# The swap of q's halves on GpSimd instead of SyncE's DMA queue, in a fused attention and ELU-MLP kernel

## The chip, the core and the metric

The kernel runs on one NeuronCore of one Trainium2 chip. The core has five engines with an instruction stream each: PE (TensorE, matmuls into PSUM), DVE (VectorE), ACT (ScalarE), POOL (GpSimd) and SP (SyncE, which here issues every DMA). Each engine works through its stream in order and waits on semaphores for the others. The metric is the device time of one execution in microseconds; less is better.

## The reference

Attention over 8 batches, 12 heads, 448 rows and 64 columns per head, with an RMS norm on q and k, followed by a two-layer MLP with ELU over the 3584 rows of 768 columns.

```python
def _attn_ref(q, k, v, g_q, g_k):
    q_n, k_n = (rmsnorm(q, g_q), rmsnorm(k, g_k))
    scores = 1.0 / np.sqrt(q.shape[-1]) * np.matmul(q_n, k_n.transpose(0, 1, 3, 2))
    attn = np.exp(scores - np.max(scores, axis=-1, keepdims=True))
    attn = attn / (np.sum(attn, axis=-1, keepdims=True) + 1e-09)
    return np.matmul(attn, v).astype(np.float32)

def _moe_ref(x, w_in, w_out):
    h = x @ w_in
    g = np.where(h > 0.0, h, np.exp(np.minimum(h, 0.0)) - 1.0)
    return (g @ w_out).astype(np.float32)
```

## The kernel before

The inputs are fp32. Every matmul operand is split into a high and a low fp16 part, so that a product is made of three fp16 products added up in PSUM.

**Pairs of heads.** The 12 heads of a batch are 6 pairs, 48 pairs in all, counted p = 0 to 47. The 896 rows of a pair (2 heads of 448) are cut into 7 tiles of 128 rows, counted T over the whole kernel. For a pair, `load_qk` (line 338) loads q and k, `qk_norm` (line 386, POOL) scales them, `k_high` and `q_high` (ACT) round them to fp16, `k_low` and `q_low` (line 414 and 421, POOL) make the rests. The high part lies in columns 0 to 63 and the rest in columns 64 to 127 of a tile of 128 columns, so that the DMA transpose of `qk_transpose` (line 429) puts high parts into partitions 0 to 63 and rests into partitions 64 to 127 of `qkt[p]`. That tile has three slots of 128 x 896 fp16: slot 0 is q, slot 1 is k, and slot 2 is q again with the two halves of the partitions exchanged. `q_swap` (lines 433 to 436) makes slot 2 out of slot 0.

**Scores.** `s_mm` (line 528) makes the scores of tile T with slot 0 against slot 1 (high times high and rest times rest in one pass) and then with slot 2 against slot 1 (the mixed products), added in the same PSUM bank. So the first tile of a pair needs the transposes for its first matmul and the swap for its second. Four PSUM banks (`s`) go round. For each T follow `s_max` (DVE, line 542), `s_exp` (ACT, 548), `s_z` (POOL, 552: a tiny instruction on the sum), `s_rec` (DVE, 559), `s_hi` (ACT, 566), `s_lo` (DVE, 571), and `s_tr` (line 581), the DMA transpose of the probabilities into `pt`. `attend` (line 592) multiplies them with v: 22 matmuls per pair.

**Weights and MLP.** `conv_in` and `conv_out` split the weights w_in (16 pieces) and w_out (24 pieces) into fp16 parts on the way; they take ACT, DVE, POOL (lines 282, 313, 322) and PE time during about the first quarter of the span. `v_mult`, `v_high`, `v_low` and `v_shift` (lines 440 to 459, POOL) prepare v. `v_shift` copies between partitions 0 to 63 and 64 to 127 on POOL: two copies of 64 x 384 fp16 per pair. The matmuls of the MLP (lines 677 and 691) begin when the first batch has its attention output, and are woven between the attention's instructions.

**Order.** The loop over half steps h (line 768) writes the order of all engines out: two half steps per tile T, 14 per pair. `at` (line 702) puts a helper's call at a half step; the MLP's matmuls are dealt out at a fixed rate (`RATE`). For p > 1 the transposes of q and of k stand at steps 4 and 6 of the pair in front, `q_swap` at 8, `v_mult` at 9. In that order the instructions reach each engine's stream; a wait of an instruction holds up all behind it on its engine.

Of the kernel before, what the change touches and what calls it, by code (L numbers as in the profile page):

```python
# [32 lines left out]
def tile_attention_then_elu_mlp(ctx: ExitStack, tc: tile.TileContext, qk, v, v_scan, gg, w_in, w_out, out):  # L33
# [13 lines left out]
    nc = tc.nc  # L47
# [15 lines left out]
    def t_mo():  # L63
# [8 lines left out]
        out=neg, in0=ident, scalar1=-1.0, scalar2=None, op0=ALU.mult  # L72
# [3 lines left out]
        out=ident, in0=ident, scalar1=2.0**UP, scalar2=None, op0=ALU.mult  # L76
# [356 lines left out]
    def q_swap(p):  # L433
        q = qkt[p]
        for a, z in ((64, 0), (0, 64)):
            nc.sync.dma_start(out=q[z : z + 64, 2], in_=q[a : a + 64, 0])

    def v_mult(p):
        n = vn[p]
# [280 lines left out]
    for p in range(NP):  # L720
        hb = HP * (p - 1)
        steps = (-20, -14, -12, -10, -8, -4, -1, -1, 1, 4, 2)
        steps = early.get(p) or [hb + h for h in steps]
        for h, fn in zip(steps, (
            load_qk, qk_square, qk_sum, qk_root, qk_newton, qk_norm, k_high, q_gain, q_high, k_low,
            q_low,
        )):

            at(-3 if p == 2 and fn == load_qk else h, fn, p)
        for h, i in ((4 if p > 1 else 6, 0), (6 if p > 1 else 8, 1)):  # L730
            at(hb + h, qk_transpose, p, i)
        at(hb + 8, q_swap, p)
        h0 = HP * p
        for h, fn in ((-2, load_v), (9, v_mult), (10, v_high), (11, v_low), (12, v_shift)):
            at(h0 + h + (5 if (p == 0) == (h > 0) and p < 2 else 0), fn, p)
        at(h0 + 22, x_high, p)
        at(h0 + 23, x_low, p)
# [125 lines left out]
```

## Time and profile before

| | |
|---|---|
| time, median of 3 runs | 1286.1 us (1285.51 to 1286.39) |
| the profiled execution | 1287.73 us, its span 1285.6 us |
| PE busy | 1191.8 us, 93% of the span |
| DVE busy | 853.3 us, 66% |
| ACT busy | 878.7 us, 68% |
| POOL busy | 529.4 us, 41%, 843 instructions |
| chain that ended last | PE 79%, ACT 6%, DVE 5%, POOL 4%, issue 3%, DMA 2% |
| swaps (line 436) | 96 DMAs of 112 KB, 2.4 us from issue to landing (median) |
| transposes of q and k (line 429) | 96 DMAs, 3.1 us from issue to landing (median) |

The span is the time from the first to the last instruction. The share of an engine is taken over the whole span, although its stages have different limits: the strip of 40 slices below shows PE at 30 to 80% in the first nine slices (one is 32 us) and at 90% or more from there on. In it a digit is the busy share in tenths, and PEclk the granted TensorE clock in tenths of full speed.

```
PE   3676578889999999999999999999999999999998
POOL 3675775665334333343344433434334334420000
PEclk9878679999999999999999999999999999999999
DMA  8999898899877897889787986799787977663011
```

### The profile page before, as it was taken

The page shows a single profiled execution, that of the slowest core. Times are in us where ns is not written, and L with a number is a line of the kernel's source. Part 1 is how long each engine was busy: PE and PEld are TensorE (multiplying, and loading weights), DVE is VectorE, ACT ScalarE, POOL GpSimd, SP SyncE. Part 2 cuts the span into 40 slices and gives each one's busy share as a digit, 9 for nine tenths or more (in the row PEclk, how much of TensorE's full clock was granted, in tenths as well). Part 3 has the DMA queues.
Part 4 walks back from the last instruction along what each step waited for, and adds up shares of the span by engine and source line. Part 5 has one row for each costly group of instructions (what it writes and reads, how often), then busy time and mean ns, then how long its engine had stood idle before and what let it go on. Part 6 is the DMA issues. An engine that isn't in the chain of part 4 may idle for free.

```text
span 1285.6 us, 21501 instructions
## 1 busy us (share of the span) xinstructions
PE 1191.8 (93%) x6976; PEld 716.4 (56%) x6976; DVE 853.3 (66%) x1913; ACT 878.7 (68%) x1889; POOL 529.4 (41%) x843
## 2 busy tenths in 40 slices
PE   3676578889999999999999999999999999999998
PEld 1333234456655765576556665576557755666576
DVE  7878779886677557856677567856785668642310
ACT  6887778985788558855797478855886578743520
POOL 3675775665334333343344433434334334420000
PEclk9878679999999999999999999999999999999999
DMA  8999898899877897889787986799787977663011
GB/s 274 224 215 239 199 224 181 199 205 236 175 147 154 203 197 142 164 166 223 149 164 157 215 176 148 155 197 203 139 169 166 219 152 171 133 147 87 1 47 62
DMA packets 452560, 219.22 MB, mean 171 GB/s; under 512 B 408673, under 2 KB 428769, under 8 KB 452449
## 3 DMA queue, kind: packets, MB, share of 16 engines
q1 hardware_dynamic: 452448, 217.86, 78.2%
q8 instruction: 55, 0.90, 0.3%
q14 instruction: 57, 0.46, 0.1%
HBM read 93.52 MB, written 14.16 MB: 84 GB/s over the span
## 4 chain that ended last, share of the span: by engine, by line
PE 79%; ACT 6%; DVE 5%; POOL 4%; issue 3%; DMA 2%; SPq 0%; ACTq 0%; POOLq 0%; DVEq 0%
PE mo L691 32%; PE mo L677 30%; PE s L535 8%; PE av L592 7%; DMA pt<-p 2%; PE mo L289 1%; ACT w32s L225 1%; ACT wts L224 1%; POOL nat L391 1%; ACT s L548 1%; POOL whi L282 1%; DVE wts L230 1%; DVE gall L571 1%; DVE st L542 1%; DVE gall L632 1%
## 5 line engine op out<-in xcount | busy, mean ns | idle before, releaser
L677 PE MATMUL mo<-x,whi 128*128 128x448 f16 x1536 | 422.8, 352 | 5.0 <-DVE e L624 5.0
L691 PE MATMUL mo<-gall,whos 128*128 128x448 f16 x1536 | 422.8, 353 | 0.7 <-DVE gall L632 0.7
L542 DVE TENSOR_REDUCE st<-s 128x1 f32<-128x448 f32 x336 | 208.4, 620 | 176.2 <-PE s L535 175.4
L552 POOL TENSOR_SCALAR st<-st 128x1 f32<-128x1 f32 x336 | 77.3, 230 | 552.4 <-ACT s L548 544.5
L691 PE MATMUL mo<-gall,wls 128*128 128x448 f16 x768 | 271.9, 354 | 0.0
L677 PE MATMUL mo<-x,wli 128*128 128x448 f16 x768 | 270.9, 353 | 0.0
L566 ACT ACTIVATE p<-s,st 128x448 f16<-128x448 f32 x294 | 185.6, 631 | 119.2 <-DMA pt<-p 99.9
L691 PEld LDWEIGHTS <-whos 128*128 128x128 f16 x1536 | 221.6, 145 | 72.3
L548 ACT ACTIVATE s<-s,st 128x448 f32<-128x448 f32 x336 | 203.2, 605 | 61.4 <-DVE st L542 58.4
L535 PE MATMUL s<-qkt 128*128 128x448 f16 (+1 forms) x768 | 188.8, 365 | 53.3 <-DVE gall L571 39.3
L677 PEld LDWEIGHTS <-whi 128*128 128x128 f16 x1536 | 150.2, 98 | 143.1 <-issue 6.9
L571 DVE SCALAR_TENSOR_TENSOR p<-s,st,p 128x448 f16<-128x448 f32 x294 | 196.4, 668 | 30.5 <-ACT p L566 28.5
L691 PEld LDWEIGHTS <-wls 128*128 128x128 f16 x768 | 110.4, 144 | 43.0 <-issue 8.4
L535 PEld LDWEIGHTS <-qkt 128*128 128x128 f16 (+1 forms) x768 | 63.2, 101 | 124.3 <-issue 62.4
L632 DVE SCALAR_TENSOR_TENSOR gall<-e,gsc,gall 128x448 f16<-128x448 f32 x128 | 100.8, 787 | 24.4 <-ACT gall L629 24.2
L677 PEld LDWEIGHTS <-wli 128*128 128x128 f16 x768 | 75.1, 98 | 74.7 <-issue 7.5
L592 PE MATMUL av<-pt,vt 128*64 128x448 f16 x1056 | 113.0, 362 | 0.1
L629 ACT ACTIVATE gall<-e,gsc 128x448 f16<-128x448 f32 x128 | 85.1, 665 | 24.3 <-DVE e L624 24.3
L599 ACT ACTIVATE x<-av 128x448 f16<-128x448 f32 x48 | 26.1, 543 | 104.4 <-PE av L592 104.4
L620 ACT ACTIVATE e<-e,nisc,isc 128x448 f32<-128x448 f32 x128 | 96.9, 757 | 0.3
L616 ACT ACTIVATE e<-mo,sc 128x448 f32<-128x448 f32 x128 | 80.6, 630 | 22.3 <-PE mo L677 22.0
L624 DVE SCALAR_TENSOR_TENSOR e<-e,mo 128x448 f32<-128x448 f32 x128 | 78.5, 613 | 16.6 <-ACT e L620 11.9
(100 smaller groups left out, 1372.6 us busy)
## 6 DMA issues: line engine op xcount, KB each, us to landing
wls<-wl_d SPq DMA_DIRECT2D x48, 512.0 KB, 3.9
nat<-in_qk SPq DMA_DIRECT2D x48, 448.0 KB, 3.9
raws<-in_w_out SPq DMA_DIRECT2D x24, 512.0 KB, 4.4
qkt<-qkt SPq DMA_DIRECT2D x96, 112.0 KB, 2.4
out<-y SPq DMA_DIRECT2D x48, 224.0 KB, 2.9
vn<-in_v SPq DMA_DIRECT2D x38, 256.0 KB, 3.7
vscan<-in_v_scan SPq DMA_DIRECT2D x36, 224.0 KB, 3.9
whos<-in_w_in SPq DMA_DIRECT2D x10, 768.0 KB, 5.5
```

Source lines behind the costliest of these rows:

```text
L535: nc.tensor.matmul(ps[r0 : r0 + n, :S], lhs, qq[:, 1, h * S : h * S + S], start=(t == 0), stop=(t == 2),)
L542: nc.vector.tensor_reduce(out=st[:, 0:1], in_=pss[T][:, :S], axis=AX.X, op=ALU.max, negate=True)
L548: nc.scalar.activation(ps, ps, AF.Exp, bias=st[:, 0:1], accum_out=st[:, 1:2])
L566: nc.scalar.activation(p16[:, :S], pss[T][:, :S], AF.Copy, scale=stats[T][:, 2:3])
L571: nc.vector.scalar_tensor_tensor(out=p16[:, S:], in0=ps[:, :S], scalar=r, in1=p16[:, :S], op0=ALU.mult, op1=ALU.subtract)
L592: nc.tensor.matmul(av[64 * h : 64 * h + 64, :S], vt[p][:, j + NJ * i, h], pt[h][:, j, :], start=(k == 0), stop=(k == len(terms) - 1),)
L616: nc.scalar.activation(e, ph[:, :S], AF.Exp, scale=sc)
L620: nc.scalar.activation(e, e, AF.Identity, scale=isc, bias=nisc)
L629: nc.scalar.activation(g[:, 0], e, AF.Copy, scale=gsc)
L632: nc.vector.scalar_tensor_tensor(out=g[:, 1], in0=e, scalar=gsc, in1=g[:, 0], op0=ALU.mult, op1=ALU.subtract)
L677: nc.tensor.matmul(ph[:, :S], w[:, c, :], x[:, r, :], start=(c == 0 and i == 0), stop=last)
L691: nc.tensor.matmul(py[:, :S], w, g[:, r, :], start=(f == 0 and i == 0), stop=last)
```

## The change

`q_swap` makes slot 2 with two copies on POOL, 64 partitions x 896 columns of fp16 each, where it issued two DMAs within SBUF on SP. The half step at which it stands is unchanged.

```diff
     def q_swap(p):
         q = qkt[p]
         for a, z in ((64, 0), (0, 64)):
-            nc.sync.dma_start(out=q[z : z + 64, 2], in_=q[a : a + 64, 0])
+            nc.gpsimd.tensor_copy(out=q[z : z + 64, 2], in_=q[a : a + 64, 0])
```

The streams of PE, DVE and ACT keep their instructions and their order. On POOL, around the swap of pair 3 (the tiny L552 are `s_z`, L440 is `v_mult`, L282 the high part of a piece of w_in):

```order
 L282 TENSOR_SCALAR whi_96<-w32s,ws 128x768
 L552 TENSOR_SCALAR st<-st 128x1 x2
+L436 COPY qkt<-qkt 64x896 x2
 L440 TENSOR_SCALAR gall<-gall,vs 128x512
 L282 TENSOR_SCALAR whi_97<-w32s,ws 128x768
```

The two copies stand between the second `s_z` and `v_mult`. On POOL, around the swap of pair 6, where w_out is being split (L313 and L322 are its `s_mult` and `s_low`):

```order
 L313 TENSOR_SCALAR w32s<-w32s,ws 128x512
 L552 TENSOR_SCALAR st<-st 128x1
+L436 COPY qkt<-qkt 64x896 x2
 L322 TENSOR_TENSOR w32s<-w32s,whos 128x512
 L440 TENSOR_SCALAR gall<-gall,vs 128x512
```

Here `s_low` and `v_mult` of the same half step stand behind the copies. The first copy waits for the transpose of q to land, as the next piece shows with its waits, in the new stream of POOL around the swap of pair 3 (DMAHW is the semaphore of a DMA, 49 its program's suffix):

```order
L552 TENSOR_SCALAR st_789<-st_789 128x1 [waits Activation_49]
L552 TENSOR_SCALAR st_810<-st_810 128x1 [waits Activation_49]
L436 COPY qkt_736<-qkt_736 64x896 [waits DMAHW6_49,PE_49,Pool_49]
L436 COPY qkt_736<-qkt_736 64x896
L440 TENSOR_SCALAR gall_130<-gall_130,vs_481 128x512 [waits Pool_49]
L282 TENSOR_SCALAR whi9_97<-w32s_133,ws_887 128x768 [waits DVE_49]
```

The wait for that transpose stood on SP before, at the DMA of line 436. On SP, at the same pair, the transposes of the probabilities that stood ahead of the swaps and behind them now follow each other:

```order
 L216 DMA raws<-in_w_in 128x1536
 L340 DMA nat<-in_qk 128x896
-L581 DMA_TRANSPOSE pt<-gall 128x7x128 x2
-L436 DMA qkt<-qkt 64x896 x2
-L581 DMA_TRANSPOSE pt<-gall 128x7x128
+L581 DMA_TRANSPOSE pt<-gall 128x7x128 x3
 L216 DMA raws<-in_w_in 128x1536
 L581 DMA_TRANSPOSE pt<-gall 128x7x128
```

SP's stream becomes shorter by the 96 issues of line 436.

## Rows read from the trace of the kernel before

**Rows 1.** The view of the windows: in each stretch of the execution (us from the span's start) its length, then the busy time of PE, PEld, DVE, ACT and POOL with the number of instructions in brackets, the granted TensorE clock, the share of the DMA engines' time and GB/s.

```profile
40.00:80.00 40.00, 27.48 (x156) 13.26 (x155) 31.91 (x73) 34.69 (x78) 27.81 (x37) 0.81 0.98 211
...
240.00:280.00 40.00, 33.67 (x228) 19.73 (x227) 36.93 (x75) 34.44 (x70) 27.23 (x32) 1.00 0.88 202
...
320.00:360.00 40.00, 40.00 (x228) 24.18 (x227) 25.99 (x68) 29.14 (x65) 14.62 (x29) 1.00 0.86 166
...
400.00:500.00 100.00, 100.00 (x586) 64.62 (x586) 65.69 (x157) 64.47 (x145) 39.51 (x71) 1.00 0.85 178
```

**Rows 2.** The view of the tile `qkt`: the issues of the swaps on SyncE with their count and their durations in ns (least, median, most), and how long PE's matmuls and weight loads of this tile sat idle until a swap had landed (us, times); then, of the view of PE's waits, the part of the matmuls alone (us, times, longest).

```profile
L436 SPq DMA_DIRECT2D qkt<-qkt x96: 472/587/1730, 15.4 to 1130.7; - x96
...
  DMA qkt<-qkt: 24.3, 12
...
PE s L535 <- DMA qkt<-qkt: 9.6, 6, 2.3
```

**Rows 3.** What GpSimd and VectorE need for one instruction: the existing copies on GpSimd from the view of the tile `vt` (least, median, most in ns); and a VectorE instruction with two SBUF operands from the view of its line (least, median, most in ns).

```profile
L459 POOL COPY vt<-vt x96: 499/502/1044, 49.4 to 1155.8; 64x384 f16<-64x384 f16 x96
...
L256 DVE SCALAR_TENSOR_TENSOR w32s<-raws,wts x30: 678/694/2405, 14.5 to 289.0; 128x512 uint32<-128x512 uint32 x24, 128x768 uint32<-128x768 uint32 x6
```

**Rows 4.** The timeline around the swap of pair 3 (start us, duration us, engine, line, operation, out<-in, count, and in brackets the idle time before it and what ended that): first SyncE, then GpSimd, then the moment at which the pair's first scores are made.

```profile
74.51 3.71 SPq L429 DMA_TRANSPOSE qkt<-t  x2
...
84.80 1.18 SPq L436 DMA_DIRECT2D qkt<-qkt  x2
...
77.65 0.19 POOL L552 TENSOR_SCALAR st<-st 128x1 f32<-128x1 f32 x1 [1.32 <-ACT s L548]
...
80.44 1.54 POOL L282 TENSOR_SCALAR whi<-w32s,ws 128x768 f16<-128x768 f32 x1 [1.81 <-DVE ws L138]
83.79 0.49 POOL L552 TENSOR_SCALAR st<-st 128x1 f32<-128x1 f32 x1 [1.81 <-ACT s L548]
...
87.83 0.19 POOL L552 TENSOR_SCALAR st<-st 128x1 f32<-128x1 f32 x1
...
87.91 0.35 PE L535 MATMUL s<-qkt 128*128 128x448 f16 x1 [1.80 <-DMA qkt<-qkt]
...
88.05 0.16 DVE L559 RECIPROCAL st<-st 128x1 f32<-128x1 f32 x1 [1.79 <-POOL st L552]
```

**Rows 5.** How long a transpose of q or k (line 429) took from its issue to its landing (us, least, median, most), of those issued in 60:80, 140:162, 162:190 and 600:700 us, in this order; of the second the row of its starts stands ahead.

```profile
DMA to landing us min/median/max: 4.4/4.7/5.0
...
L429 SPq DMA_TRANSPOSE qkt<-t x2: 1227/1385/1543, 147.0 to 148.9; - x2
...
DMA to landing us min/median/max: 3.9/4.2/4.6
...
L429 SPq DMA_TRANSPOSE qkt<-t x2: 1226/1656/2086, 172.5 to 174.4; - x2
...
DMA to landing us min/median/max: 5.6/6.0/6.5
...
DMA to landing us min/median/max: 2.9/2.9/3.1
```

**Rows 6.** The timeline of GpSimd around the new places of the swaps of pairs 6 and 7, what ScalarE waited for behind the second, and one instruction of GpSimd behind the swap of pair 9 (columns as in rows 4).

```profile
151.43 1.16 POOL L322 TENSOR_TENSOR w32s<-w32s,whos 128x512 f16<-128x512 f32 x1 [0.33 <-ACT whos L318]
...
155.78 0.60 POOL L552 TENSOR_SCALAR st<-st 128x1 f32<-128x1 f32 x1 [1.38 <-ACT s L548]
...
161.94 0.19 POOL L552 TENSOR_SCALAR st<-st 128x1 f32<-128x1 f32 x1
...
175.69 0.19 POOL L552 TENSOR_SCALAR st<-st 128x1 f32<-128x1 f32 x1 [0.82 <-ACT s L548]
...
181.15 0.19 POOL L552 TENSOR_SCALAR st<-st 128x1 f32<-128x1 f32 x1
...
183.78 0.63 ACT L566 ACTIVATE p<-s,st 128x448 f16<-128x448 f32 x1 [3.70 <-DMA pt<-p]
...
238.42 1.06 POOL L313 TENSOR_SCALAR w32s<-w32s,ws 128x512 f32<-128x512 f32 x1 [1.78 <-DVE ws L138]
```

**Rows 7.** The timeline in the long even part, around the swap of pair 23: SyncE's transposes, GpSimd's instructions around the swap's new place (columns as in rows 4).

```profile
612.08 2.61 SPq L429 DMA_TRANSPOSE qkt<-t  x2
...
614.00 0.19 POOL L552 TENSOR_SCALAR st<-st 128x1 f32<-128x1 f32 x1 [1.61 <-ACT s L548]
...
619.03 0.19 POOL L552 TENSOR_SCALAR st<-st 128x1 f32<-128x1 f32 x1 [3.70 <-ACT s L548]
```

**Rows 8.** The timeline of pair 0 (columns as in rows 4).

```profile
15.40 1.17 SPq L436 DMA_DIRECT2D qkt<-qkt  x2
...
17.20 1.69 POOL L391 TENSOR_TENSOR nat<-nat,r 128x896 f32<-128x896 f32 x1 [5.68 <-issue]
```

**Rows 9.** The chain that ended last, pieces in order of time (start us, duration us, what): the 22 matmuls of one pair's output (line 592) at three places.

```profile
56.66 2.25 PE av L592 x22
...
150.22 4.29 PE av L592 x22
...
174.97 3.91 PE av L592 x22
```

**Rows 10.** The view of the windows again, with the columns of rows 1, for the stretch of the last of these pieces and the one behind it.

```profile
160.00:180.00 20.00, 10.96 (x67) 5.08 (x68) 15.53 (x42) 14.56 (x32) 13.63 (x19) 0.54 0.93 193
180.00:200.00 20.00, 18.40 (x121) 9.83 (x120) 16.39 (x33) 16.30 (x34) 14.82 (x18) 1.00 0.89 203
```

## The prediction

> **What bounds the kernel now.** I read the windows first: in each stretch, which engine is busy all the time. From 320 us on PE is busy in every microsecond at full clock, in 320:360 as in 400:500, while POOL works 14.6 of 40 and 39.5 of 100 us [rows 1]. There nothing but PE's own instructions sets the time, and these don't change. Before that no engine is full: PE works 27.5 of 40 us in 40:80 and 33.7 in 240:280, where DVE works 36.9 [rows 1]. So only what happens in about the first 300 us, while the weights are being split, can move the end; what is lost or won by then goes into the time one to one, since PE afterwards works off a fixed list.
>
> Next the view of the tile that the change touches, to see who waits for a swap: PE, 12 times, 24.3 us with its weight loads, the matmuls alone 6 times and 9.6 us [rows 2]. Weight loads and matmuls wait at the same moments, so 9.6 us is the figure for PE. That is what a sooner swap could win at most.
>
> Third the timeline of all engines at one such wait, to see whether PE is alone in waiting. At pair 3 PE waits 1.80 us for the swap until 87.91. In the same moment DVE's reciprocal has waited 1.79 us, until 88.05, for the tiny `s_z` on POOL, which stood from 83.79 on behind other work of POOL and came at 87.83 [rows 4]. DVE is in order: had PE been ready sooner, the maximum over the new scores would have stood behind that reciprocal all the same. The wait for the swap lies beside a wait for POOL.
>
> **What the change removes.** 96 issues on SP, a pair of them 1.18 us at pair 3 [rows 4], and the DMAs' landing. The swap was late because SP reached it late: the transposes of pair 3 were issued from 74.51 on, the swap at 84.80 [rows 4]. POOL reaches it at 77.84 (77.65 and 0.19). PE's wait of 1.80 us goes; what is late next at that place is POOL's `s_z` at 87.83, so I book 0 us for it, with 9.6 us as the far bound. The 1.18 us of SP bring the probabilities' transposes behind the swap forward, but the wait for such a transpose that I see on ACT, 3.70 us until 183.78 [rows 6], is for one issued ahead of the swap. I book 0 for that too.
>
> **What it adds on POOL.** No row shows a copy of 64 x 896. The nearest is `v_shift`'s copy of 64 x 384, which takes 0.50 us [rows 3]. In proportion that is 0.50 x 896 / 384 = 1.17 us; with the 0.19 us of `s_z`, an instruction on one column [rows 4], as the fixed part, it is 0.19 + 0.31 x 896 / 384 = 0.92 us. I take 0.92, since a part of 0.19 is seen to be fixed: 1.84 us a swap, 88 us over 96 copies. The same existing copy has taken up to 1.044 us [rows 3], so a disturbed copy can be twice as long and a swap 3.7 us. DVE's instructions with two SBUF operands stretch too: line 256 takes 0.69 us mostly and has taken 2.4 [rows 3].
>
> The Trainium skill, GPSIMD Engine Reference, section "1. Specifications", says that GpSimd's way to SBUF is shared with VectorE and contended when a DVE instruction reads two SBUF inputs. The trace agrees as far as the two maxima go (1.044 us and 2.4 us); by that rule copies that fall beside lines 230, 256 and 632 cost both engines, which is the second case below. The same page, section "3.1 Elementwise", gives 1.03 cycles per element at 1.2 GHz for a light body; an estimate from that is 0.77 us per copy and 1.54 us for a swap, and the sum below would be 0.6 us smaller by it, 0.3 for each of the two pairs where it isn't hidden.
>
> It adds a wait as well: POOL now stands still until the transpose of q has landed, and `v_mult`, a weight piece and the next `s_z` stand behind it; for `s_z` wait DVE's reciprocal and then the whole row of tiles. So place by place:
>
> - Pair 3. The first transpose is issued at 74.51 [rows 4] and lands 4.4 to 5.0 us later [rows 5], at 78.9 to 79.5, while POOL is free at 77.84: 1.1 to 1.7 us of wait, and 1.84 of copies, 2.9 to 3.5 in all. POOL's idle time between there and `s_z` at 83.79 is 1.81 + 1.81 = 3.6 us [rows 4]. Hidden: 0, and 1.8 late if both copies double (1.7 + 3.7 - 3.6). I take the same for pairs 4 and 5, which have the same instructions.
> - Pair 6. Issue at 147.0, landing 3.9 to 4.6 later [rows 5], at 150.9 to 151.6; POOL is free at 151.10 (151.43 less its idle 0.33). So up to 0.5 of wait and 1.84, against idle 0.33 + 1.38 = 1.7 until `s_z` at 155.78 [rows 6]. That leaves 0.1 to 0.6 us, and 2.5 if the copies double. From 155.78 to 161.94 no idle time stands in POOL's rows [rows 6], so it goes through: 0.4.
> - Pair 7. Issue at 172.5, landing 5.6 to 6.5 later, at 178.1 to 179.0 [rows 5]; POOL is free at 175.88 [rows 6], waits 2.2 to 3.1 us and copies until 180.0 to 180.9. Three weight and v instructions follow, which I put at 1 us each by the 1.16 us of one at pair 6 [rows 6]; `s_z`, at 181.15, comes some 2 us later. It is needed by the ACT instruction of line 566, which until 183.78 waits for a DMA anyway [rows 6]; I book 0.2, from 0 to 1.
> - Pairs 8 to 10. By the one row that I show, POOL waits 1.78 us for DVE behind the swap of pair 9 [rows 6], which covers 1.84 but for 0.06. I book 0; up to 0.5 each where a copy falls beside DVE's instructions with two operands.
> - Pairs 11 to 47. At pair 23 the transposes are issued at 612.08 and land 2.9 us later, at 615.0; POOL has done `s_z` at 614.19 and waits for ACT for 3.70 us until 619.03 [rows 5, 7]. 0.8 of wait and 1.84 of copies fit, and PE is full there. 0.
> - Pairs 0 to 2. For pair 0 the swap is issued at 15.40, on the transpose's landing, and POOL's next instruction starts at 17.20 [rows 8]: two copies end at 17.24, just in time. Beside the first stand two-operand instructions of DVE; with one copy doubled (0.92 more) the norm of pair 1, which heads the chain there, is 0.8 late. From 0 to 1.9. Pairs 1 and 2 I take as pair 3: 0.
>
> The sum is 0.8 + 0.4 + 0.2 = 1.4 us: 1287.7 of the profiled execution becomes 1289.1. That execution is 1.6 us above the median of 1286.1, on which I put the same 1.4: 1287.5 us. A measurement of this kernel tells a change from none from about 0.2%, 2.6 us, on: faster below 1283.5, slower above 1288.7. So the forecast is no change.
>
> **The rivals.**
>
> - Port and wait (slower). The copies, doubled by what DVE does beside them, and the wait for q's transpose, overflow POOL's idle time in each of the early pairs. Price: 1.9 at pair 0, 1.8 at pair 3 and less at 4 and 5, say 0.6 each, 2.5 at pair 6, and 1 at pair 7, together 8.4; with half of these met, 4.2 to 6: 1290.3 to 1292. For it: the chain of POOL from 83.79 on has no slack, and the maxima of rows 3. Against: the idle 3.6 us ahead of it. It decides once a swap takes over 3.6 us on POOL at pairs 3 to 5.
> - The swap was on the path (faster). If the 9.6 us of PE's waits were not beside POOL's but ahead of it, half of them would give 4.8: 1281.3. For it: the waits are real, one in each early pair, and PE, at 27.5 of 40 us, could use them. Against: the 0.14 us between 87.91 and 88.05.
> - The clock (either sign). The 22 matmuls of a pair's output took 2.25 us at 56.66, but 4.29 and 3.91 at 150.22 and 174.97 [rows 9], where the granted clock of 160:180 is 0.54, much of it at 1.2 GHz, ahead of a stretch at 2.4 [rows 10]; PE was busy 11.0 of 20 us there and 18.4 behind it. A small shift in time may move such stretches. If both regain full clock, 2.0 + 1.7 = 3.7 us are won: 1282.4; if two others fall to the lower, 4 are lost: 1290.1.
>
> **How the numbers follow.** No change as above 0.50; port and wait 0.27; swap on the path 0.10; the clock 0.13, of that 0.07 faster. Faster is 0.10 + 0.07 = 0.17, same 0.50, slower 0.27 + 0.06 = 0.33. The range runs from between the two faster cases, 1282, to the far end of the slower one, 1292; beyond it lie half of the faster cases and some of the slower, under 2 in 10.
>
> **What would show it.** Right: line 436 stands on POOL with 96 copies of about 0.92 us; in the waits PE has none for a swap; POOL's busy time is 617 us; PE is again full from about 300 us on; the reciprocal still waits for `s_z` at pairs 3 to 5. Wrong: the even part of PE begins over 2.6 us sooner or later, copies near 1.8 us, a wait of DVE for POOL that has grown by more than a microsecond a pair, or PE idle behind 320 us, which would mean that POOL's wait for the transposes reaches PE in the long part too.

## The result, and where the profile after shows it

The changed kernel takes 1294.56 us (median of 4 runs, 1294.24 to 1295.37) against 1286.24 us for the kernel before, measured beside it (median of 4 runs, 1285.51 to 1288.6): ratio 1.0063, 95% interval 1.0051 to 1.0075, 8 us slower. The forecast was no change, 1287.5 us, with a range up to 1292. The profiled execution of the changed kernel took 1294.24 us with a span of 1292.5, against a span of 1285.6 before.

The windows of the changed kernel, with the columns of [rows 1]:

```profile
40.00:80.00 40.00, 25.51 (x148) 13.04 (x149) 31.29 (x70) 32.63 (x73) 31.11 (x38) 0.79 0.84 182
240.00:280.00 40.00, 34.81 (x241) 19.28 (x241) 34.28 (x75) 36.38 (x75) 29.55 (x35) 1.00 0.89 201
320.00:360.00 40.00, 40.00 (x238) 25.32 (x237) 24.88 (x67) 25.45 (x57) 20.46 (x34) 1.00 0.93 186
400.00:500.00 100.00, 100.00 (x580) 64.68 (x578) 65.53 (x153) 67.58 (x149) 47.13 (x80) 1.00 0.80 175
```

PE is full in 320:360 and in 400:500 as before, although POOL works there longer than in [rows 1]. In 40:80 PE works 25.5 us in place of 27.5, and POOL 31.1 in place of 27.8: the time is lost early.

The view of the tile `qkt`: the copies (least, median, most in ns), what POOL waited for ahead of them, and PE's weight loads and matmuls that now wait for a swap (us, times):

```profile
L436 POOL COPY qkt<-qkt x96: 926/928/1576, 15.5 to 1132.0; 64x896 f16<-64x896 f16 x96
...
  DMA qkt<-t: 20.7, 18
...
  PEld L535: 1.0, 1
  PE s L535: 0.4, 1
```

A copy takes 0.928 us (median), and PE's waits for a swap, 24.3 us in [rows 2], are gone but for 1.4. So the change does what it says. And yet the work falls behind. This table holds the start of a pair's attention sum (the first matmul of line 592) in the timelines of four kernels (us). The swap of pair p+2 stands near the sum of pair p: in the last column from 1.7 us ahead of it (pair 2) to 3.2 us behind it (pair 10). The last two columns are experiments of the next section: only pair 0 on GpSimd, and only pairs 2 to 10.

| sum of pair | before | after | pair 0 alone | pairs 2 to 10 |
|---|---|---|---|---|
| 0 | 56.59 | 60.62 | 58.92 | 56.74 |
| 1 | 79.83 | 82.59 | 80.62 | 79.63 |
| 2 | 102.79 | 108.36 | 104.20 | 103.29 |
| 3 | 127.64 | 133.72 | 128.60 | 128.64 |
| 4 | 150.15 | 156.24 | 151.12 | 151.15 |
| 5 | 174.91 | 181.87 | 175.62 | 176.91 |
| 6 | 203.28 | 210.17 | 203.40 | 205.40 |
| 7 | 232.88 | 240.46 | 233.02 | 235.71 |
| 9 | 290.29 | 298.50 | 290.44 | 293.74 |
| 11 | 337.11 | 344.94 | 337.21 | 340.19 |

After is 4.0 us late at the first sum, 6.1 at the fifth, 8.2 at the tenth, and no later from there on. A single trace of the early part is not exact to a microsecond: two traces of one and the same kernel (the first experiment below, run twice) differ by 2.2 us at the sum of pair 2 and by 1.2 at that of pair 9.

The swaps of pairs 3, 6 and 0 in the timelines of the changed kernel (columns as in [rows 4]), the first for [rows 4], the second for [rows 6], the third for [rows 8]:

```profile
83.69 2.53 POOL L436 COPY qkt<-qkt 64x896 f16<-64x896 f16 x2 [1.42 <-DMA qkt<-t]
...
92.41 0.19 POOL L552 TENSOR_SCALAR st<-st 128x1 f32<-128x1 f32 x1
...
92.63 0.17 DVE L559 RECIPROCAL st<-st 128x1 f32<-128x1 f32 x1 [2.13 <-POOL st L552]
...
157.69 2.36 POOL L436 COPY qkt<-qkt 64x896 f16<-64x896 f16 x2 [0.51 <-DMA qkt<-t]
...
163.15 0.19 POOL L552 TENSOR_SCALAR st<-st 128x1 f32<-128x1 f32 x1
...
163.37 0.16 DVE L559 RECIPROCAL st<-st 128x1 f32<-128x1 f32 x1 [0.33 <-POOL st L552]
...
15.50 2.54 POOL L436 COPY qkt<-qkt 64x896 f16<-64x896 f16 x2 [4.00 <-DMA qkt<-t]
18.78 2.49 POOL L391 TENSOR_TENSOR nat<-nat,r 128x896 f32<-128x896 f32 x1 [0.73 <-DVE a_in L132]
...
16.20 1.87 DVE L377 SCALAR_TENSOR_TENSOR ss<-ss,r 128x14 f32<-128x14 f32 x2
...
18.31 0.23 DVE L381 TENSOR_SCALAR r<-r,kap 128x7 f32<-128x7 f32 x1
```

At pair 6 the `s_z` that waited 1.38 us for ACT in [rows 6] now waits for nothing: POOL is late, and DVE's reciprocal waits for it. At pair 3 the reciprocal waits 2.13 us where it waited 1.79 [rows 4]. At pair 0 the norm of pair 1 starts at 18.78, 1.6 us later than in [rows 8], and two tiny VectorE instructions beside the copies take 1.87 us. The copies end at 18.04, 0.8 us behind the norm's old start; the other 0.7 us (0.73 in brackets) the norm waits for VectorE, which makes the norm's second input `r` in the two held instructions and in the one of line 381. These two rows of the kernel before show the same instructions without a hold:

```profile
16.22 0.38 DVE L377 SCALAR_TENSOR_TENSOR ss<-ss,r 128x14 f32<-128x14 f32 x2
...
16.84 0.23 DVE L381 TENSOR_SCALAR r<-r,kap 128x7 f32<-128x7 f32 x1
```

Taken together, DVE's waits for `s_z` between 17 and 300 us have hardly grown (us, times, longest; before, then after):

```profile
DVE st L559 <- POOL st L552: 10.4, 8, 1.9
...
DVE st L559 <- POOL st L552: 11.1, 9, 2.1
```

So the lateness isn't a longer wait at that one place. It shows in the chain that ended last: of the 30 us of the stretch 150:180 POOL's work held 8.4 before and holds 21.2 after, with 5.0 more of POOL's wait for q's transpose, while PE's share fell from 10.0 us to nothing.

Three causes can be read into this: GpSimd's own time (the copies push all behind them on GpSimd back, `s_z` among it), its wait for q's transpose, and the time for which a copy holds VectorE. The experiments take them apart for pairs 2 to 10, and in part for pair 0. Ratios are to the kernel before, measured beside each run, with a median of 1287.1 to 1287.2; a thousandth is 1.3 us.

### The profile page after: what moved, and what is told of

The parts are those of the page before. It is cut to its first block, busy times and chain, and to the rows that moved or that the text cites. A ratio compares the mean times of both kernels' runs of the same rounds, so it can differ in the third digit from the quotient of the medians.

```text
span 1292.5 us, 21450 instructions
## 1 busy us (share of the span) xinstructions
PE 1192.4 (92%) x6976; PEld 716.9 (55%) x6976; DVE 855.3 (66%) x1913; ACT 884.4 (68%) x1889; POOL 624.7 (48%) x939
## 4 chain that ended last, share of the span: by engine, by line
PE 78%; POOL 4%; ACT 4%; DVE 4%; issue 2%; DMA 1%; POOLq 0%; ACTq 0%; DVEq 0%
PE mo L691 33%; PE mo L677 30%; PE s L535 8%; PE av L592 7%; POOL w32s L322 1%; DMA qkt<-t 1%; DVE gall L632 1%; ACT w32s L225 1%; ACT s L548 1%; DVE wts L230 1%; DVE w32s L256 1%; POOL nat L391 1%; ACT wts L224 1%; POOL w32s L313 0%; PE mo L289 0%
## 5 line engine op out<-in xcount | busy, mean ns | idle before, releaser
L552 POOL TENSOR_SCALAR st<-st 128x1 f32<-128x1 f32 x336 | 76.0, 226 | 455.4 <-ACT s L548 411.7
L632 DVE SCALAR_TENSOR_TENSOR gall<-e,gsc,gall 128x448 f16<-128x448 f32 x128 | 97.6, 762 | 24.1 <-ACT gall L629 24.1
L436 POOL COPY qkt<-qkt 64x896 f16<-64x896 f16 x96 | 92.1, 960 | 28.0 <-DMA qkt<-t 20.7
```

The costliest lines, as they stand in the source:

```text
L436: nc.gpsimd.tensor_copy(out=q[z : z + 64, 2], in_=q[a : a + 64, 0])
L632: nc.vector.scalar_tensor_tensor(out=g[:, 1], in0=e, scalar=gsc, in1=g[:, 0], op0=ALU.mult, op1=ALU.subtract)
```

## The experiments: which pairs

All but one edit `q_swap`, and that one moves it. In the diffs, which are cut to what matters, DMA stands for the line with the transfer of the kernel before, COPY for the line with the copy of the changed one. Letters of theories in the expectations are explained where they first occur; B, C and D fell with the first three experiments, A was split into what follows it.

**Pairs 11 to 47 by copies.**

```diff
-            COPY
+            DMA if p < 11 else COPY
```

> Pairs 0 to 10 by DMA as before, pairs 11 to 47 by copies on GpSimd (74 of the 96 copies). Theory A, all of the loss falls into the first 11 pairs, before TensorE is full: 1285 to 1287 us, the time of the kernel before, or up to 1 us under it. Rival B, the copies cost something in every pair (loss in proportion to their number, 74/96 of 8.3): 1292 to 1293 us. Rival C, the loss comes from GpSimd being too busy in the even part, where DVE's reciprocals wait for it: 1294 us.

Measured: 1285.39 us, ratio 0.999 (0.998 to 0.9999). The long part loses nothing, so the loss stems from the first eleven pairs.

**Pairs 0 to 10 by copies.**

```diff
-            COPY
+            COPY if p < 11 else DMA
```

> The counterpart: pairs 0 to 10 by copies on GpSimd (22 copies), pairs 11 to 47 by DMA. Theory A: 1294 to 1296 us, the whole loss and none of the 0.4 to 1.3 us that the part behind gave back. Rival B: 1288 us. Rival C: 1286 us.

Measured: 1294.43 us, 1.0059 (1.0044 to 1.0074): the whole loss, from 22 of 96 copies.

**Pairs 0 and 1 by DMA.**

```diff
-            COPY
+            DMA if p < 2 else COPY
```

> Only pairs 0 and 1 by DMA, pairs 2 to 47 by copies on GpSimd. Theory A as read from the changed kernel's trace (pair 0 2.1 us and pair 1 0.9 us, each the time for which a small VectorE instruction stood until a copy ended): 1291 to 1292 us, and the two VectorE instructions back at 0.38 us for two and 0.23 us. Rival D, the shifts at pairs 0 and 1 are slack that a later wait would have swallowed anyway: 1294 us. Rival B: 1294 us.

Measured: 1290.0 us, 1.0024 (1.0014 to 1.0034). Two pairs carry 0.0039, 5 us, more than the 3 us of the rows; the two small VectorE instructions of pair 0 are back at 0.37 us together, the one of pair 1 at 0.23.

**Pair 0 by DMA.**

```diff
-            COPY
+            DMA if p < 1 else COPY
```

> Only pair 0's swap by DMA, pairs 1 to 47 by copies on GpSimd. With pairs 0 and 1 by DMA the time was 1290.0 us. Theory A, with the shifts read at GpSimd's rows (2.1 us at pair 0, 0.9 us at pair 1): about 1291 to 1292 us, so that pair 0 alone carries the greater part of the 4.6 us. Rival, both pairs alike: 1292.3 us. Rival, pair 1 carries it (its held instruction stands in front of every later VectorE step): 1294 us.

Measured: 1291.57 us, 1.0035 (1.0023 to 1.0046): pair 0 takes 0.0028 of the 0.0039, 3.6 us. The 0.0011 that are left for pair 1 lie within the two intervals.

**Pair 0 alone by copies.**

```diff
-            COPY
+            COPY if p < 1 else DMA
```

> Pair 0's swap alone by two copies on GpSimd, the other 47 by DMA. From the ratios of the changed kernel (1.0063) and of the one with pair 0 by DMA (1.0035): plus 3.6 us on the kernel before, ratio 1.0028. By the shift at GpSimd's rows alone, 2.1 us: 1.0016. If a later wait swallows it: 1.000.

Measured: 1288.38 us, 1.001 (1.0001 to 1.0019). A third of the expected price. The table shows why: 2.3 us late at the first sum, 0.1 at the seventh. The pairs further on make the shift of pair 0 good when they have no copies. In the times, 0.0010 alone and 0.0028 beside the other copies are just within their errors of each other, so whether the prices of the pairs add up isn't shown.

**Pairs 2 to 10 alone by copies.**

```diff
-            COPY
+            COPY if 2 <= p <= 10 else DMA
```

> Pairs 2 to 10 by copies on GpSimd, pairs 0, 1 and 11 to 47 by DMA. If the prices of the pairs add up: 1.0024 (pairs 2 to 47 by copies) with nothing for pairs 11 to 47, so 1.002 to 1.0035. If pairs 2 to 10 only cost something because pairs 0 and 1 had already spent the slack: under 1.001.

Measured: 1291.96 us, 1.0034 (1.0023 to 1.0046): 4.4 us, half of the loss, without any help from pairs 0 and 1. Its column in the table falls back by 0.7 us behind the swap of pair 3 (from -0.2 to +0.5), 0.5 behind pair 4, 1.0 behind pair 6, 0.7 behind pair 8 and 0.6 behind pairs 9 and 10, and by nearly nothing behind pairs 2, 5 and 7. The sum of pair 8, which the table leaves out, is at 264.64 against 261.82, 2.8 late as the one ahead of it, so the 0.6 are pair 10's.

**Pairs 6 to 10 alone by copies.**

```diff
-            COPY
+            COPY if 6 <= p <= 10 else DMA
```

> Pairs 6 to 10 by copies on GpSimd, all others by DMA. By the steps at which the attention sums fall behind with pairs 2 to 10 on GpSimd (pair 3 0.5, pair 4 0.5, pair 6 1.0, pair 8 0.7, pair 10 0.6 us): 2.3 of 3.4 us, ratio 1.0015 to 1.0025. If pairs 2 to 5 had first used up the slack: under 1.001. By the prediction's own prices (pair 6 0.4, pair 7 0.2): 1.0005.

Measured: 1290.53 us, 1.0023 (1.0012 to 1.0034), 3 us, which the prediction had priced at 0.6. The steps behind pairs 6, 8 and 10 are there again in this trace, 0.9, 0.7 and 0.7 us; in the first trace with pairs 0 to 10 by DMA they are -1.2, 0.0 and 0.0. Behind pairs 3 and 4 that trace has steps of 1.1 and 0.5 without any copy, so theirs above can't be told from chance.

## The experiments: what in them costs

**Copies that nobody needs, in all pairs, beside the DMAs.**

```diff
             DMA
+        for a, z in ((64, 0), (0, 64), (64, 0)):
+            nc.gpsimd.tensor_copy(out=dum[z : z + 64], in_=dum[a : a + 64])
```

The tile `dum` is made and set to zero once, ahead of it.

> The swap by DMA as in the kernel before, and on top of it, at the same place of GpSimd's queue, three copies of 64x534 within a tile that nothing else reads (about 0.63 us each by the line through 0.50 us for 384 columns and 0.93 us for 896, so 1.88 us a swap, as much as the two copies). They wait for nothing. Theory A with the wait (copies that start late because q's transpose is late, pair 0 at 15.5 us in the middle of VectorE's small instructions, and 0.2 to 1.5 us in pairs 3 to 7): pair 0 runs in GpSimd's idle time and costs nothing, about half of the loss goes: 1288 to 1291 us. Rival F, GpSimd's sheer time: 1294 us or more. Rival E, the missing DMAs: 1286 us.

Measured: 1292.27 us, 1.0039 (1.0025 to 1.0054). That lies above the 1288 to 1291 us of the theory with the wait and below the 1294 of GpSimd's sheer time: copies that wait for nothing and replace no DMA cost over half of the loss, and 0.0024 are left for the wait and for pair 0's bad moment, which this run doesn't have: its copies of pair 0 start at 11.30 us, and the norm of pair 1 at 16.97.

**The same in pairs 2 to 10 only.**

```diff
             DMA
+        if 2 <= p <= 10:
+            for a, z in ((64, 0), (0, 64), (64, 0)):
+                nc.gpsimd.tensor_copy(out=dum[z : z + 64], in_=dum[a : a + 64])
```

> All swaps by DMA, and in pairs 2 to 10 three copies of 64x534 on GpSimd on top, which nothing reads and which wait for nothing (2.0 us a swap). Theory H, GpSimd's own time is what costs there: 1.002 to 1.0035, as with the real copies in these pairs (1.0034). Rival W, the wait for q's transpose costs (some 5 us of idle GpSimd in pairs 3 to 7): 1.000 to 1.001.

Measured: 1291.76 us, 1.0033 (1.002 to 1.0045), the same as with the real copies in these pairs (1.0034). So in pairs 2 to 10 neither the wait for q's transpose nor the missing transfers cost anything that can be measured here, where the two intervals leave room for some 2 us: it is GpSimd's time. At pair 6 alone, one trace of each, the step is 0.6 us without the wait and 1.0 with it.

**One of the two copies in pairs 2 to 10.**

```diff
-            COPY
+            COPY if 2 <= p <= 10 and a == 0 else DMA
```

> In pairs 2 to 10 one of the two copies on GpSimd, the other by DMA; the other pairs by DMA. GpSimd waits for q's transpose as with two copies, and has 0.93 us a swap in place of 1.86. Theory H: about half, 1.001 to 1.002. Rival W: 1.003 as with both copies.

Measured: 1288.43 us, 1.0008 (0.9998 to 1.0017). It waits for the transpose as the pair of copies does, and costs a quarter, less than theory H had said (1.001 to 1.002), with an interval from nothing to half.

**Copies in seven pieces, in pairs 2 to 10.**

```diff
-            COPY
+            if 2 <= p <= 10:
+                for j in range(NJ):
+                    nc.gpsimd.tensor_copy(out=q[z : z + 64, 2, j], in_=q[a : a + 64, 0, j])
+            else:
+                DMA
```

> In pairs 2 to 10 the two copies cut into fourteen of 64x128 (4.2 us of GpSimd a swap in place of 1.86), the other pairs by DMA. Theory H: in proportion to GpSimd's time at least, 1.007 to 1.009. Rival P, VectorE being held for a whole copy (0.93 us, with a piece 0.3 us) is what costs: under 1.003.

Measured: 1301.83 us, 1.0114 (1.01 to 1.0128). With 0.93, 1.86 and 4.2 us of GpSimd a swap the nine pairs cost 1.0, 4.4 and 14.7 us: more than in proportion, since the first part of it falls into idle time. Were the hold of VectorE the cause, pieces would have helped. What the hold adds also stands in VectorE's busy time over the execution: 853.3 us before, 857.4 with the two copies in pairs 2 to 10, 854.2 with the copies that nobody needs there, and 854.1 with pieces, where the time is 14.7 us longer.

**Copies in seven pieces, in all pairs.**

```diff
-            COPY
+            for j in range(NJ):
+                nc.gpsimd.tensor_copy(out=q[z : z + 64, 2, j], in_=q[a : a + 64, 0, j])
```

> Each copy cut into seven of 64x128 (by the same line 0.29 us each, 4.0 us a swap in place of 1.86). If a copy holds VectorE from its start to its own end and no longer, the two VectorE instructions that stood 1.87 us (pair 0, two of them) and 0.94 us (pair 1) end with a piece: under 1.0 and 0.5 us. If VectorE stands until GpSimd has no copy left, 3 us and more. The time: GpSimd's time is 2.1 us a swap more. If the loss is the hold alone, 1290 us or less; if it is GpSimd's time in the first pairs, 1300 us or more.

Measured: 1303.11 us, 1.0125 (1.011 to 1.014), on the side of GpSimd's time. For the hold itself, four rows of the timelines, all of pair 1 but the third: a VectorE instruction on seven columns that stands beside a copy of 64 x 896 (the changed kernel, with the copies ahead), of 64 x 534 (the run with copies that nobody needs), then the two of pair 0 and the one of pair 1 beside pieces of 64 x 128.

```profile
35.42 1.90 POOL L436 COPY qkt<-qkt 64x896 f16<-64x896 f16 x2
35.43 0.94 DVE L381 TENSOR_SCALAR r<-r,kap 128x7 f32<-128x7 f32 x1
...
33.56 0.65 DVE L381 TENSOR_SCALAR r<-r,kap 128x7 f32<-128x7 f32 x1
...
15.83 0.50 DVE L377 SCALAR_TENSOR_TENSOR ss<-ss,r 128x14 f32<-128x14 f32 x2
...
35.89 0.31 DVE L381 TENSOR_SCALAR r<-r,kap 128x7 f32<-128x7 f32 x1
```

0.94, 0.65 and 0.31 us, where copies take 0.93, 0.63 and 0.29, and 0.23 us with no copy beside it: VectorE stands until the copy that runs has ended, and no longer. The hold is real, but in pairs 2 to 10 it is not what costs.

**Pair 0 alone, in pieces.**

```diff
-            COPY
+            if p == 0:
+                for j in range(NJ):
+                    nc.gpsimd.tensor_copy(out=q[z : z + 64, 2, j], in_=q[a : a + 64, 0, j])
+            else:
+                DMA
```

> The same with pair 0's two copies cut into fourteen of 64x128 (4.2 us in all, the two VectorE instructions at 0.50 us in place of 1.87). If what costs in pair 0 is that VectorE is held: near the kernel before, 1.000 to 1.001. If what costs is GpSimd's own lateness (its product of k starts at 20.05 us in place of 18.78 and 17.20): 1.003 to 1.004, and more than with two copies.

Measured: 1291.62 us, 1.0031 (1.002 to 1.0042), more than with two copies. In the timelines of both kernels the norm of pair 1 starts so, first with two copies, then with fourteen pieces:

```profile
18.75 2.49 POOL L391 TENSOR_TENSOR nat<-nat,r 128x896 f32<-128x896 f32 x1 [0.74 <-DVE a_in L132]
...
20.46 1.69 POOL L391 TENSOR_TENSOR nat<-nat,r 128x896 f32<-128x896 f32 x1
```

VectorE is free of the hold here (the two instructions take 0.38 us), and GpSimd's own time makes the norm 1.7 us later than two copies do. So GpSimd's time costs in pair 0 as well. It is not all of the price of two copies there: in the first row, as in the changed kernel, about half of the norm's lateness of 1.6 us is the wait for the held VectorE. No run has the two copies at this place without the hold.

**The copies two half steps later.**

```diff
-        at(hb + 8, q_swap, p)
+        at(hb + 10, q_swap, p)
```

> The copies on GpSimd issued two half steps later (at 10 in place of 8), behind a product and a copy of v that GpSimd has anyway; pairs 3 to 7 then no longer wait for q's transpose (20.7 us, 18 times before). Theory A: 1291.5 to 1293 us, since the loss of pairs 0 and 1 stays (4.6 us) and the waits of pairs 3 to 7 go. Rival F, GpSimd's sheer time: 1294.5 us, since the waits only moved GpSimd's idle time. Rival G: the scores now wait for the swap, 1295 us or more.

Measured: 1302.31 us, 1.0121 (1.0104 to 1.0138). The expectation of theory A failed; rival G's, 1295 us or more, holds, with nearly twice its 8 us. At pair 3, and in the view of the waits from 17 to 300 us (us, times, longest):

```profile
90.84 0.49 POOL L552 TENSOR_SCALAR st<-st 128x1 f32<-128x1 f32 x1 [1.65 <-ACT s L548]
...
92.09 1.90 POOL L436 COPY qkt<-qkt 64x896 f16<-64x896 f16 x2
...
96.95 0.19 POOL L552 TENSOR_SCALAR st<-st 128x1 f32<-128x1 f32 x1
...
94.04 0.36 PE L535 MATMUL s<-qkt 128*128 128x448 f16 x1 [0.88 <-POOL qkt L436]
...
DVE st L559 <- POOL st L552: 23.5, 12, 4.1
...
PE s L535 <- POOL qkt L436: 5.3, 5, 1.6
```

The wait for the transpose is gone there, but the copies now stand behind the `s_z` that ends POOL's idle time, in the stretch without any; from one `s_z` to the next it takes 6.1 us, where [rows 4] have 4.04. DVE's waits for `s_z` are 23.5 us, against 11.1 in the changed kernel, and PE's matmuls wait 5.3 us for a swap, against 0.4. So the idle 3.6 us ahead of that `s_z` [rows 4], on which the prediction counted, do cover most of the swap of pair 3, but only work that stands ahead of it. How the loss divides between the later `s_z` and the later swap, no run shows.

**Copies on VectorE, in all pairs.**

```diff
-            nc.gpsimd.tensor_copy(out=q[z : z + 64, 2], in_=q[a : a + 64, 0])
+            nc.vector.tensor_copy(out=q[z : z + 64, 2], in_=q[a : a + 64, 0])
```

> All 96 copies on VectorE instead of GpSimd, at the same place of the program. It takes the DMAs away as the change does, but GpSimd has the work that it had before. Theory A, the loss is GpSimd's copies (the held VectorE and the overflow of GpSimd): under 1294, about 1289 us, because each copy of some 0.3 to 0.6 us stands in VectorE's own queue and waits there for q's transpose (0.2 to 1.4 us in pairs 3 to 7). Rival E, the loss comes from taking the 96 transfers off the queue of SP (other order of the DMAs, another clock of TensorE): 1294 us here too.

Measured: 1287.45 us, 1.0003 (0.9993 to 1.0013). A copy takes 0.39 us there:

```profile
L436 DVE COPY qkt<-qkt x96: 385/389/799, 15.3 to 1130.3; 64x896 f16<-64x896 f16 x96
```

96 transfers gone and nothing lost beyond the noise: the missing DMAs are not the cause.

**Pairs 0 and 1 by DMA, the others on VectorE.**

```diff
-            COPY
+            DMA if p < 2 else nc.vector.tensor_copy(out=q[z : z + 64, 2], in_=q[a : a + 64, 0])
```

> Pairs 0 and 1 by DMA, pairs 2 to 47 by copies on VectorE. With all 48 pairs on VectorE the ratio was 1.0003, while its first pairs ran as late as those of the changed kernel (60.2 us against 56.6 at the first attention sum). If pairs 0 and 1 cost as much there as on GpSimd (0.0039): 0.996 to 0.998, faster than the kernel before. If what VectorE does in pairs 2 to 10 costs as much as on GpSimd: 1.002 or more. If the first pairs' loss was made good behind them: 1.000.

Measured: 1286.2 us, 0.9993 (0.9985 to 1.0002). No gain that can be told from none: with pairs 0 and 1 on VectorE too it was 1.0003. By the expectation that means a loss of the first pairs that was made good behind them, which no trace shows: the one trace with all copies on VectorE is of its slowest execution, 1291.41 us, and there the work is 3.6 us late at the first sum and still 4.6 at the twelfth.

**Pairs 0 and 1 by DMA, 2 to 10 on VectorE, the others on GpSimd.**

```diff
-            COPY
+            eng = nc.vector if p < 11 else nc.gpsimd
+            DMA if p < 2 else eng.tensor_copy(out=q[z : z + 64, 2], in_=q[a : a + 64, 0])
```

> Pairs 0 and 1 by DMA, pairs 2 to 10 by copies on VectorE, pairs 11 to 47 by copies on GpSimd. Theory H, GpSimd's time is what costs in pairs 2 to 10: 0.998 to 1.000, against 1.0024 with these pairs on GpSimd. Rival, it is taking the transfers out of these pairs that costs: 1.002 or more.

Measured: 1286.01 us, 0.9991 (0.9982 to 1.0). Against 1.0024 with pairs 2 to 10 on GpSimd: the engine makes the difference.

**The first experiment once more, the version that beats both kernels.**

```diff
-            COPY
+            DMA if p < 11 else COPY
```

> Pairs 0 to 10 by DMA, pairs 11 to 47 by copies on GpSimd, in five rounds. If the copies gain something where TensorE is full: 0.998 to 0.9995. If they do nothing there: 0.9995 to 1.0005.

Measured: 1285.05 us, 0.9987 (0.9978 to 0.9995), with 0.999 the first time: some 1.5 us faster than the kernel before. But 1.0063 and 1.0059, with copies and with DMAs in pairs 11 to 47, show no such gain. In the trace of this run the lead over the kernel before is 1.4 us at the sum of pair 5 and 1.5 at that of pair 10, and the first swap that differs stands behind the sum of pair 9. So it isn't shown that copies gain anything where PE is full; where the lead comes from stays open.

## Why the prediction was wrong

The step that failed is the sum of the places: the prediction let POOL's idle time cover the copies in all of the first eleven pairs but for 0.8, 0.4 and 0.2 us, 1.4 in all, and 8.3 were measured. Pairs 2 to 10, booked at 0.6, cost 4.4 us, through GpSimd's plain time; pairs 0 and 1, booked at 0.8, cost 5 us beside the others (each to within some 1.5 us), where in pair 0 the hold of VectorE adds a wait that the prediction didn't have. The steps one by one:

- **PE full from 320 us on, only the first 300 us count.** Right: the loss is complete at the tenth sum, and pairs 11 to 47 cost nothing that can be measured.
- **PE's waits for the swap, booked at 0.** Right. The 9.6 us of the matmuls are gone, and PE's matmuls wait 9.1 us more for DVE's instruction of line 571, behind the reciprocal of line 559 that the prediction had seen waiting at the same moment (before, then after):

```profile
PE s L535 <- DVE gall L571: 39.3, 20, 4.0
...
PE s L535 <- DVE gall L571: 48.4, 21, 4.0
```

With pairs 2 to 10 on VectorE, where no time is lost, it is 47.2 us from 17 to 300 us: the wait has only changed its name.

- **0.92 us a copy, 88 us in all.** Right: 0.928 us, 92.1 us in all. Stretched copies are rare: over 96 x 0.928 = 89.1 us the 96 have 3 us. Pairs 0 and 3 have one each, of 1.58 and 1.57 us.
- **Pairs 3 to 5, hidden.** Nearly: the swap of pair 3 took 1.42 + 2.53 = 3.95 us against 3.6 of idle, 0.35 over. What that costs stays open: with pairs 2 to 10 alone the sums fell back by 0.7 and 0.5 behind pairs 3 and 4, no more than a trace without copies there shows, and by nothing behind pair 5.
- **Pair 6, 0.4.** Undersized. With pairs 2 to 10 alone the wait took 0.72 and the copies 2.27 us against 1.7 of idle, and the next sum fell back by 1.0.
- **Pairs 8 to 10, booked at 0 by one row of pair 9.** Of the places this is the one that failed outright, and by the prediction's own method. The rows of pairs 8 and 10 were there to be read; in the timeline of the kernel before, POOL behind the places of these two swaps:

```profile
204.88 1.16 POOL L322 TENSOR_TENSOR w32s<-w32s,whos 128x512 f16<-128x512 f32 x1 [0.24 <-ACT whos L318]
...
207.44 0.70 POOL L313 TENSOR_SCALAR w32s<-w32s,ws 128x512 f32<-128x512 f32 x1 [0.72 <-DVE ws L138]
208.68 0.41 POOL L552 TENSOR_SCALAR st<-st 128x1 f32<-128x1 f32 x1 [0.54 <-ACT s L548]
...
268.03 1.06 POOL L313 TENSOR_SCALAR w32s<-w32s,ws 128x512 f32<-128x512 f32 x1 [1.14 <-DVE ws L138]
269.17 0.19 POOL L552 TENSOR_SCALAR st<-st 128x1 f32<-128x1 f32 x1
```

Idle time up to the next `s_z` is 0.24 + 0.72 + 0.54 = 1.5 us at pair 8 and 1.14 at pair 10, against 1.84 of copies: 0.3 and 0.7 by the prediction's own method. With pairs 2 to 10 on GpSimd the same places read as follows (the edit moves the lines by three: L439 is the copy, L555 is `s_z`):

```profile
206.83 1.90 POOL L439 COPY qkt<-qkt 64x896 f16<-64x896 f16 x2
...
211.40 0.50 POOL L555 TENSOR_SCALAR st<-st 128x1 f32<-128x1 f32 x1
...
267.85 1.90 POOL L439 COPY qkt<-qkt 64x896 f16<-64x896 f16 x2
...
272.86 0.19 POOL L555 TENSOR_SCALAR st<-st 128x1 f32<-128x1 f32 x1
```

No idle time is left, and the sums behind fall back by 0.7 and 0.6 us.

- **Pair 7, 0.2, and pairs 2, 5 and 9.** Right to within 0.2 with pairs 2 to 10 alone.
- **Pair 0, 0.8, pair 1, 0.** Too low: 1.3 us with pair 0 alone, and 3.6 with copies in all the others. One copy did stretch (by the prediction's own figures a doubled one makes 0.96 us, not 0.8), and the copies end 0.8 us behind the norm's old start as booked. Left out was the other way: the copies hold the VectorE instructions that make `r`, and the norm waits another 0.7 us for it. Pair 1 adds 1.0035 - 1.0024, 1.4 us, within the noise. Each place was priced as if those behind it kept all their idle time to make a shift good; that copies in pairs 2 to 10 spend this slack is argued from the two columns of the table, and no run shows it by itself.
- **Rival "port and wait".** Its full price, 8.4 us, is what was measured, by luck: it put 1.9 us on pairs 0 and 1 and 3.0 on pairs 3 to 5, and nothing on pairs 8 to 10. Its main statement holds: POOL's idle time overflows in the early pairs. But in pairs 2 to 10 neither the wait for q's transpose (1.0033 without, 1.0034 with it) nor the hold of VectorE (VectorE's busy time grew by 0.8 us where 14.7 were lost) decides. GpSimd's plain 1.86 us a swap does; a small share of the other two isn't excluded. At pair 0 the hold has a share.
- **The sign of a wait of DVE for POOL that grows by over a microsecond a pair.** It didn't come (10.4 to 11.1 us in all), though the prediction was wrong; the sign of an even part that begins over 2.6 us late did.
- **Rival clock.** Not needed. The granted clock of the kernel before and of the one with pairs 11 to 47 by copies, first run, in 40:60 and 100:120 (columns as in [rows 1]):

```profile
40.00:60.00 20.00, 13.63 (x86) 6.62 (x83) 16.37 (x39) 17.22 (x39) 14.27 (x19) 0.87 0.97 223
100.00:120.00 20.00, 13.96 (x89) 7.07 (x88) 16.57 (x37) 15.78 (x34) 13.37 (x17) 0.83 0.99 250
...
40.00:60.00 20.00, 13.36 (x82) 6.67 (x80) 15.12 (x37) 15.71 (x34) 14.34 (x19) 0.81 1.05 219
100.00:120.00 20.00, 15.67 (x91) 7.64 (x90) 17.35 (x36) 15.59 (x34) 12.45 (x18) 0.77 1.05 256
```

The second has the lower clock in both and loses nothing. The changed kernel has 0.78 and 0.76 there, which may be a part of its lateness at those places; no run separates that. It doesn't carry the loss: over 50:300 the granted clock is 0.86 before, 0.84 in the changed kernel, and 0.85 in the run with pieces in pairs 2 to 10, which lost 14.7 us.

## What to carry to other kernels

Idle time of an in-order engine covers new work only if it lies between the new work and the next instruction that others wait for; add it up for every place where the work is put, one row for several places is a guess. Since idle time covers only the first part of it, the cost of added work rises faster than the work (1.0, 4.4 and 14.7 us for one copy, two copies and fourteen pieces). Ask not only what the engine itself is late with, but also whom its new instructions hold. Where a small transfer leaves a critical stretch, put its replacement on an engine that does it in less time there (0.39 us on VectorE cost nothing that could be measured here), or leave it on the queue.

## What the runs showed of the hardware

A VectorE instruction on 128 x 7 elements with one SBUF tensor as input (0.23 us) took 0.94, 0.65 and 0.31 us when it came just behind the start of a GpSimd copy of 0.93, 0.63 and 0.29 us. The prediction had thought of instructions with two SBUF inputs alone. Who comes second stands, on either side: in [rows 8] the norm on GpSimd took 1.69 us, and 2.49 in the changed kernel, where a VectorE instruction of line 256 started 0.01 us ahead of it and took 0.95; in the kernel before that instruction came 0.10 us behind the norm, and took 2.40.

The Trainium skill, SBUF — State Buffer, section "Who interferes with whom", says that VectorE and GpSimd share one port pair as an exclusive lock, which whoever issues first holds for the whole instruction, and that a `tensor_scalar` can take it too. The three durations agree with it to 0.03 us.

GpSimd's copies of 64 x 128, 384, 534 and 896 fp16 elements took 0.29, 0.50, 0.63 and 0.93 us (medians); an estimate from these four is 0.18 us and 0.83 ns a column. VectorE's of 64 x 896 took 0.39.
